# The low three bits of the weights: from VectorE to GpSimd

## The chip, the cores and the metric

The kernel runs on one core of one Trainium2 chip. The metric is the device time of one execution in microseconds (us). The engines are named as the profile names them: PE (TensorE, products), PEld (its weight loads), DVE (VectorE), ACT (ScalarE), POOL (GpSimd) and SP (SyncE, which here only issues the DMAs).

## What is computed

The reference reads the weights as float64 and everything else as float32. Cross-attention between 8 x 8 blocks of 512 tokens and 32 state slots comes first, then a feed-forward layer with a rational activation.

```python
scores = scale * np.matmul(x, state.transpose(0, 1, 3, 2))
a = np.exp(scores - scores.max(-1, keepdims=True)); a /= a.sum(-1, keepdims=True) + 1e-09
xread = np.matmul(a, state)                  # sread: the same with the roles exchanged
h = concat([xread, sread], 2) @ w_in         # w_in: 512 x 2048, float64
P = a0 + a1*h + a2*h**2 + a3*h**3
Q = 1 + |b0|*|h| + |b1|*h**2
out = (P / (Q + 1e-6)) @ w_out               # w_out: 2048 x 512, float64
```

[...]

## The kernel before, in words

The hidden width of 2048 is cut into 8 blocks (u = 0 to 7) of 256. Nine token blocks (b = 0 to 8: eight times 512 tokens, then the state rows) times 8 blocks of width give 72 steps n = 8b + u. The chain of one step is: PE makes h (token `F`, line 755); ACT and DVE make numerator and denominator (`FC` and `FB` on ACT, `mu`, `po` and `qd` on DVE, which read h in PSUM); ACT takes the reciprocal through a logarithm and an exponential (`qa`, `ln`, `ex`); DVE and POOL make the activation as a high and a low part (`g1`, `g2` and `g3` on DVE, `gl` on POOL); PE multiplies both with `w_out` (`mh`, `ml`, line 828).

The conversion of the weights takes place in the first 120 us or so, woven between steps 0 to 7. The 16 groups of raw weights are numbered k = 0 to 15: groups 0, 1, 2, 4, 6, 8, 10 and 12 are blocks of `w_in`, the others blocks of `w_out`. For each group the raw words are loaded (`lr`, SP), ACT makes `cv_y` (`cp`, line 325), DVE makes `cv_r` from the low words (`jr`, lines 333 to 342, in two halves of 512 columns for groups 0 to 4 and in one piece of 1024 after that), and DVE joins them (`jl`, line 351). A block of `w_in` goes into `win_sb`, from which PE makes the extra products `X` (line 659: state times `w_in`). Their results are copied out of PSUM by ACT (`XA`, `fA`) or DVE (`XV`) and stored. A block of `w_out` is split into a high part (cast by ACT, line 362) and a remainder, which POOL subtracts (`sp`, line 363; for groups 13 and 14 DVE does it, `sv`).

The order of the work is written out by hand: the list `ORDER` is a string of tokens, and each engine gets its instructions in the order of the tokens. Every engine works through its own list in order; an instruction that waits holds up all that stand behind it on that engine. The h tiles and the results of the extra products share two buffers in PSUM (`ps_h`, tag `h`), so an extra product can begin only when the tile two places before it has been read. The tag `cv` has four buffers for `cv_y` and `cv_r`, the tag `raw` two.

Around the conversion POOL has, in its order: the subtraction of the row maxima of batch 0 (`row_sup`, line 503), the row scaling (`row_norm`, line 544), the remainder of group 3 (`sp:3`), then `gl` of a step and `sp` of a group in turns, later the low part of the attention matrix (`a_lp`, line 574) and the split of the weights of the later steps (`fs`, line 708).

Of the kernel before, what the change touches and what calls it, by code (L numbers as in the profile page):

```python
# [183 lines left out]

class Tagged:


    def __init__(self, ctx, tc, bufs):  # L190
        self.bufs = bufs
        self.pools = {
            t: ctx.enter_context(tc.tile_pool(name=t, bufs=n)) for t, n in bufs.items()
        }

    def tile(self, shape, dtype, name, tag, bufs=None):
        return self.pools[tag].tile(shape, dtype, name=name, tag=tag)
# [3 lines left out]
def attention_rational_ffn(  # L201
# [22 lines left out]
    cp = ctx.enter_context(tc.tile_pool(name="cp", bufs=1))  # L224
    ld = ctx.enter_context(tc.tile_pool(name="ld", bufs=2))
    at = Tagged(
        ctx,
        tc,
        dict(e1=1, mx=2, sT=1, cm=2, rs=2, e2T=1, e2=1, r2=2, aT=2, sr=2),
    )  # L230
    cv = ctx.enter_context(tc.tile_pool(name="cv", bufs=4))
    ew = Tagged(ctx, tc, dict(xo=2, m=2, A=3, C=3, L=2, gh=2, gl=2))
    wp = ctx.enter_context(tc.tile_pool(name="wp", bufs=1))
    wo = wp.tile([P, 2, U * 2, DM], F32R, name="wo")
    ps_o = ctx.enter_context(tc.tile_pool(name="ps_o", bufs=1, space=PSUM))
    ps_h = ctx.enter_context(tc.tile_pool(name="ps_h", bufs=2, space=PSUM))
# [121 lines left out]
    def conv_split(k, eng):  # L358
        _, u = groups[k]
        m = CV[k][1].bitcast(F32)  # L360
        f = slice(2 * u, 2 * u + 2)
        nc.scalar.copy(wo[:, 0, f, :], m)  # L362
        eng.tensor_tensor(  # L363
            wo[:, 1, f, :], m, wo[:, 0, f, :].bitcast(F32), op=ALU.subtract
        )

    def load_win(n):
        t = ld.tile([P, NP, CW], F32, name="win_sb", tag="win", bufs=3)
        nc.sync.dma_start(t, w_in32[n % U])
        win_t[n] = t  # L370
# [74 lines left out]
    def col_max(b, j=None):  # L445
        cm = once(b, "cm", at_tile("cm", [P, 2], 2))
# [82 lines left out]
    def row_sum(b, j=None):  # L529
        rs = once(b, "rs", at_tile("rs", [P, NT * 8], 2))  # L530
# [136 lines left out]
    def extra_out(i, copy):  # L667
# [4 lines left out]
        else:  # L672
            t = ew.tile([P, 2, 2, CW], F32, name="xo", tag="xo", bufs=2)
# [18 lines left out]
    def load_m(n):  # L692
        t = cv.tile([P, 2, 2, CW], F32, name="m_sb", tag="raw", bufs=2)
# [10 lines left out]
    def fold_split(n):  # L704
# [115 lines left out]
    def mm(n, t, parts, place):  # L820
# [51 lines left out]
    def sread_hi():  # L872
        t = cv.tile([P, 2, NP, B * NS], F32R, name="sh", tag="raw", bufs=2)
# [7 lines left out]
    def keep_warm(k):  # L881
# [8 lines left out]
        "jr": join_rest,  # L890
        "jl": join_low,
# [4 lines left out]
        "fs": fold_split,  # L896
# [106 lines left out]
```

## Time and profile before

| | |
|---|---|
| median of 3 runs | 664.8 us (664.68 to 665.32) |
| span of the profiled execution, first to last instruction | 662.6 us |
| what lies around the span (median less span) | 2.2 us |
| PE busy | 645.4 us, 97% |
| DVE busy | 617.8 us, 93% |
| ACT busy | 513.4 us, 77% |
| POOL busy | 319.0 us, 48% |

The span is the profiled execution's own time between its first and last instruction; the time that a run reports also holds what lies around it. A busy engine is one that has an instruction under way. For PE the end of an instruction is a model, so that a busy PE need not be at its peak; a gap between its instructions is a real wait. A timeline row gives start, duration, engine, line, operation, output and inputs, and in brackets the idle time just before it with the engine that ended it.

### The profile page before, as it was taken

The page shows a single profiled execution, that of the slowest core. Times are in us where ns is not written, and L with a number is a line of the kernel's source. Part 1 is how long each engine was busy: PE and PEld are TensorE (multiplying, and loading weights), DVE is VectorE, ACT ScalarE, POOL GpSimd, SP SyncE. Part 2 cuts the span into 40 slices and gives each one's busy share as a digit, 9 for nine tenths or more (in the row PEclk, how much of TensorE's full clock was granted, in tenths as well). Part 3 has the DMA queues.
Part 4 walks back from the last instruction along what each step waited for, and adds up shares of the span by engine and source line. Part 5 has one row for each costly group of instructions (what it writes and reads, how often), then busy time and mean ns, then how long its engine had stood idle before and what let it go on. Part 6 is the DMA issues. An engine that isn't in the chain of part 4 may idle for free.

```text
span 662.6 us, 11126 instructions
## 1 busy us (share of the span) xinstructions
PE 645.4 (97%) x4442; PEld 504.8 (76%) x4442; DVE 617.8 (93%) x586; ACT 513.4 (77%) x604; POOL 319.0 (48%) x172
## 2 busy tenths in 40 slices
PE   5899999999999999999999999999999999999997
PEld 3355555778887888788887888787878888888995
DVE  5898899999989999999999999999999899999885
ACT  5888988887777888787778778787888678875663
POOL 1234442554654556645555454635545446464531
PEclk9999999999999999999999999999999999999999
DMA  8989897350330512132215022231225101111301
GB/s 332 393 304 355 303 344 264 125 190 8 105 113 20 187 48 96 32 121 83 71 43 180 13 96 63 86 138 33 95 81 174 33 0 48 63 48 65 97 1 63
DMA packets 28984, 81.46 MB, mean 123 GB/s; under 512 B 2820, under 2 KB 2948, under 8 KB 28932
## 3 DMA queue, kind: packets, MB, share of 16 engines
q1 hardware_dynamic: 28932, 80.75, 34.9%
q8 instruction: 35, 0.57, 0.3%
q14 instruction: 17, 0.14, 0.1%
HBM read 52.95 MB, written 27.79 MB: 122 GB/s over the span
## 4 chain that ended last, share of the span: by engine, by line
PE 84%; ACT 0%; DVE 0%; issue 0%
PE h L755 28%; PE o__1655 L828 2%; PE o__5714 L828 2%; PE o__1696 L828 2%; PE o__5193 L828 2%; PE o__3485 L828 2%; PE o__2273 L828 2%; PE o__4639 L828 2%; PE o__4009 L828 2%; PE o__2839 L828 2%; PE o__3455 L828 2%; PE o__2301 L828 2%; PE o__1681 L828 2%; PE o__5754 L828 2%; PE o__4014 L828 2%; PE o__2850 L828 2%
## 5 line engine op out<-in xcount | busy, mean ns | idle before, releaser
L818 POOL TENSOR_TENSOR gl<-C,L 128x1024 fp32r<-128x1024 f32 (+1 forms) x70 | 173.1, 2473 | 235.6 <-DVE C L811 155.9
L755 PE MATMUL h<-aT,m 128*128 128x512 f32 x736 | 193.4, 409 | 0.7 <-ACT xo L675 0.6
L755 PEld LDWEIGHTS h<-aT,m 128*128 128x128 f32 x736 | 137.2, 188 | 42.8 <-issue 12.2
L767 ACT ACTIVATE C<-h,cst 128x1024 f32<-128x1024 f32 (+1 forms) x72 | 83.2, 1156 | 47.6 <-PE h L755 35.6
L708 POOL TENSOR_TENSOR m<-m_sb,m 128x512 fp32r<-128x512 f32 x56 | 80.1, 1435 | 56.2 <-ACT m L707 37.4
L774 ACT ACTIVATE A<-h,cst 128x1024 f32<-128x1024 f32 (+1 forms) x72 | 76.7, 1065 | 30.6 <-PE h L755 26.3
L799 DVE SCALAR_TENSOR_TENSOR gh<-C,cst,L 128x1024 fp32r<-128x1024 f32 (+1 forms) x72 | 90.3, 1254 | 6.1 <-ACT L L870 2.3
L788 DVE SCALAR_TENSOR_TENSOR A<-A,b0a,h 128x1024 f32<-128x1024 f32 (+1 forms) x72 | 87.1, 1215 | 7.8 <-ACT A L774 6.6
L811 DVE SCALAR_TENSOR_TENSOR C<-C,cst,A 128x1024 f32<-128x1024 f32 (+1 forms) x72 | 89.4, 1241 | 2.2
L782 DVE SCALAR_TENSOR_TENSOR C<-C,cst,h 128x1024 f32<-128x1024 f32 (+1 forms) x72 | 87.7, 1219 | 2.1
L805 DVE SCALAR_TENSOR_TENSOR A<-A,gh 128x1024 f32<-128x1024 f32 (+1 forms) x72 | 87.7, 1218 | 1.7
L778 DVE TENSOR_TENSOR C<-C,h 128x1024 f32<-128x1024 f32 (+1 forms) x72 | 82.8, 1152 | 5.9 <-ACT C L767 4.0
L794 ACT ACTIVATE A<-A 128x1024 f32<-128x1024 f32 (+1 forms) x72 | 72.6, 1011 | 19.5 <-DVE A L788 19.5
L860 ACT ACTIVATE L<-A 128x1024 f32<-128x1024 f32 (+1 forms) x72 | 73.0, 1013 | 3.6 <-ACT A L794 0.4
L870 ACT ACTIVATE L<-L 128x1024 f32<-128x1024 f32 (+1 forms) x72 | 72.8, 1013 | 1.6
L659 PE MATMUL ps_x<-win_sb,st 64*32 64x256 f32 x1024 | 34.5, 388 | 4.2 <-DVE win_sb L351 2.5
L707 ACT CAST m<-m_sb 128x512 fp32r<-128x512 f32 x56 | 34.0, 613 | 0.1
L659 PEld LDWEIGHTS ps_x<-win_sb,st 64*32 64x32 f32 x1024 | 17.5, 107 | 17.2 <-issue 5.1
L755 PEld LDWEIGHTS h<-sh,m 128*128 128x128 f32 x192 | 24.2, 191 | 0.7
L755 PE MATMUL h<-sh,m 128*128 128x256 f32 x192 | 24.4, 283 | 0.0
L363 POOL TENSOR_TENSOR wo<-cv_r,wo 128x1024 fp32r<-128x1024 f32 x6 | 15.4, 2565 | 16.2 <-ACT wo L362 16.2
L544 POOL TENSOR_TENSOR e<-e,rs 128x512 f32<-128x512 f32 x13 | 13.9, 1085 | 12.4 <-DVE rs L538 12.4
(262 smaller groups left out, 1121.4 us busy)
## 6 DMA issues: line engine op xcount, KB each, us to landing
m_sb<-m_dram SPq DMA_DIRECT2D x28, 512.0 KB, 4.7
m_dram<-xo SPq DMA_DIRECT2D x20, 512.0 KB, 4.4
out_dram<-o_sb SPq DMA_DIRECT2D x34, 256.0 KB, 4.4
xT_sb<-in_xT_dram SPq DMA_DIRECT2D x16, 512.0 KB, 5.0
x_sb<-in_x_dram SPq DMA_DIRECT2D x16, 512.0 KB, 6.4
raw<-in_w_out_dram SPq DMA_DIRECT2D x14, 512.0 KB, 6.8
raw<-in_w_in_dram SPq DMA_DIRECT2D x12, 512.0 KB, 6.8
w_in_dram<-win_sb SPq DMA_DIRECT2D x8, 512.0 KB, 5.9
```

The source lines that it names most:

```text
L708: nc.gpsimd.tensor_tensor(m[:, 1], t, m[:, 0].bitcast(F32), op=ALU.subtract)
L755: nc.tensor.matmul(h[:, ci * W : (ci + 1) * W], l, r, start=(q == 0), stop=(q == len(seq) - 1),)
L767: nc.scalar.activation(e["C"], e["h"], AF.Identity, scale=cst[:, 3:4], bias=cst[:, 2:3])
L774: nc.scalar.activation(e["A"], e["h"], AF.Abs, scale=cst[:, 5:6])
L778: nc.vector.tensor_tensor(e["C"], e["C"], e["h"], op=ALU.mult)
L782: nc.vector.scalar_tensor_tensor(e["C"], e["C"], cst[:, 1:2], e["h"], op0=ALU.add, op1=ALU.mult)
L788: nc.vector.scalar_tensor_tensor(e["A"], e["A"], b0a, e["h"], op0=ALU.add, op1=ALU.mult)
L799: nc.vector.scalar_tensor_tensor(e["gh"], e["C"], cst[:, 0:1], e["L"], op0=ALU.add, op1=ALU.mult)
L805: nc.vector.scalar_tensor_tensor(e["A"], e["A"], 1.0 + 1e-6, e["gh"].bitcast(F32), op0=ALU.add, op1=ALU.mult)
L811: nc.vector.scalar_tensor_tensor(e["C"], e["C"], cst[:, 0:1], e["A"], op0=ALU.add, op1=ALU.subtract)
L818: eng.tensor_tensor(e["gl"], e["C"], e["L"], op=ALU.mult)
L828: nc.tensor.matmul(O[t], e[l][:, j * W + t * P : j * W + (t + 1) * P], wo[:, k, 2 * u + j, :], start=(place == FIRST[n // U, t] and i + j ...
```

## The change

All 21 tokens `jr` in `ORDER` become `jp`, at the same places in the string. `jp` calls the same function with `nc.gpsimd` as the engine. There the product with 2^-29 and the minimum with 7 become a product with 0.92 * 2^-29 and a sum with 0.139, which also ends at 7 when rounded. The tile `cv_r` of a group is now taken from the four `cv` buffers when its bits are made, and no longer when `cv_y` is. The rest of the diff moves the numbers of buffers into one table and adds a token (`ft`) that `ORDER` does not use.

```diff
-    "... row_exp:0:0 jr:0:1 lr:3 cp:1:1 ls:2:8 lr:2 col_max:0:1 "
+    "... row_exp:0:0 jp:0:1 lr:3 cp:1:1 ls:2:8 lr:2 col_max:0:1 "
...
+    def conv_tile(k, w):
+        if (k, w) not in CV:
+            CV[k, w] = cv.tile(
+                [P, 2, 2 * CW], I32, name=("cv_y", "cv_r")[w], tag="cv"
+            )
+        return CV[k, w]
+
     def conv_parts(k, j=None):
-        if k not in CV:
-            CV[k] = [
-                cv.tile([P, 2, 2 * CW], I32, name=name, tag="cv", bufs=4)
-                for name in ("cv_y", "cv_r")
-            ]
...
-    def join_rest(k, j=None):
+    def join_rest(k, j=None, eng=None):
         js = slice(0, 2) if j is None else slice(j, j + 1)
-        nc.vector.tensor_scalar(
-            CV[k][1][:, js],
+        (eng or nc.vector).tensor_scalar(
+            conv_tile(k, 1)[:, js],
             raw_words(k, j, 0),
-            2.0**-29,
-            7.0,
+            0.92 * 2.0**-29,
+            0.139,
             op0=ALU.mult,
-            op1=ALU.min,
+            op1=ALU.add,
         )
...
         "jr": join_rest,
+        "jp": lambda k, j=None: join_rest(k, j, nc.gpsimd),
```

In the listings of the order that follow, a line number of the kernel after is some 9 above that of the kernel before. POOL at the start, in the kernel before (`e_153` is the attention matrix of batch 0, `cv_r` and `wo` of the third row belong to group 3):

```order
L503 TENSOR_TENSOR e_153<-e_153,mx 128x512 x2
L544 TENSOR_TENSOR e_153<-e_153,rs 128x512 x2
L363 TENSOR_TENSOR wo<-cv_r,wo 128x1024
L818 TENSOR_TENSOR gl<-C,L 128x1024
L363 TENSOR_TENSOR wo<-cv_r,wo 128x1024
```

The same place after:

```order
L511 TENSOR_TENSOR e_153<-e_153,mx 128x512
L344 TENSOR_SCALAR cv_r<-raw 128x512 x2
L511 TENSOR_TENSOR e_153<-e_153,mx 128x512
L344 TENSOR_SCALAR cv_r<-raw 128x512 x2
L552 TENSOR_TENSOR e_153<-e_153,rs 128x512 x2
L344 TENSOR_SCALAR cv_r<-spare 128x512 x2
L372 TENSOR_TENSOR wo<-cv_r,wo 128x1024
L344 TENSOR_SCALAR cv_r<-spare 128x512 x4
L344 TENSOR_SCALAR cv_r<-raw 128x1024
L826 TENSOR_TENSOR gl<-C,L 128x1024
```

The two halves of group 3 stand ahead of the subtraction of group 3 (L372); the four halves behind it are those of group 2 and then of group 4, and the whole piece is group 5.

DVE at the same place, before (the first join is that of group 3, the second, into `win_sb`, that of group 2; `C` and `h` belong to step 0):

```order
L335 TENSOR_SCALAR cv_r<-spare 128x512 x2
L351 SCALAR_TENSOR_TENSOR cv_r<-cv_y,cv_r 128x1024
L335 TENSOR_SCALAR cv_r<-spare 128x512
L512 TENSOR_SCALAR r_200<-r_200 128x2
L516 RECIPROCAL r_200<-r_200 128x2
L335 TENSOR_SCALAR cv_r<-spare 128x512
L351 SCALAR_TENSOR_TENSOR win_sb<-cv_y,cv_r 128x1024
L778 TENSOR_TENSOR C<-C,h 128x1024
```

After:

```order
L360 SCALAR_TENSOR_TENSOR cv_r<-cv_y,cv_r 128x1024
L520 TENSOR_SCALAR r_199<-r_199 128x2
L524 RECIPROCAL r_199<-r_199 128x2
L360 SCALAR_TENSOR_TENSOR win_sb<-cv_y,cv_r 128x1024
L786 TENSOR_TENSOR C<-C,h 128x1024
```

The bits have left DVE, and the join of group 2 still stands ahead of the first product of step 0.

POOL near the end of the conversion, before (`m` is the first split of later weights, step 8; the last row is the subtraction of group 15):

```order
L818 TENSOR_TENSOR gl<-C,L 128x1024
L574 TENSOR_TENSOR aT<-eT,aT 128x1024
L708 TENSOR_TENSOR m<-m_sb,m 128x512
L818 TENSOR_TENSOR gl<-C,L 128x1024
L363 TENSOR_TENSOR wo<-cv_r,wo 128x1024
```

After (from the bits of group 13 on):

```order
L344 TENSOR_SCALAR cv_r<-raw 128x1024
L552 TENSOR_TENSOR e_857<-e_857,rs 128x512
L344 TENSOR_SCALAR cv_r<-raw 128x1024
L826 TENSOR_TENSOR gl<-C,L 128x1024
L344 TENSOR_SCALAR cv_r<-raw 128x1024
L582 TENSOR_TENSOR aT<-eT,aT 128x1024
L716 TENSOR_TENSOR m<-m_sb,m 128x512
L344 TENSOR_SCALAR cv_r<-raw 128x1024
L826 TENSOR_TENSOR gl<-C,L 128x1024
L372 TENSOR_TENSOR wo<-cv_r,wo 128x1024
```

The bits of groups 13, 12, 14 and 15 stand here, those of group 12 behind a row scaling and those of group 15 behind the split of step 8.

## Rows read from the trace of the kernel before

**Rows 1.** The page: busy time of PE over the whole span.

```profile
PE 645.4 (97%) x4442; PEld 504.8 (76%) x4442; DVE 617.8 (93%) x586; ACT 513.4 (77%) x604; POOL 319.0 (48%) x172
```

**Rows 2.** Stretches: length, then busy us and instructions by engine, granted PE clock, DMA.

```profile
20.00:120.00 100.00, 95.58 (x1223) 55.20 (x1211) 92.74 (x92) 88.58 (x102) 35.20 (x14) 0.98 0.87 320
120.00:640.00 520.00, 519.98 (x2895) 427.04 (x2894) 497.87 (x449) 403.64 (x471) 275.76 (x146) 1.00 0.24 80
```

**Rows 3.** The page's costliest groups: the extra products, idle before them by releaser.

```profile
L659 PE MATMUL ps_x<-win_sb,st 64*32 64x256 f32 x1024 | 34.5, 388 | 4.2 <-DVE win_sb L351 2.5
```

**Rows 4.** DVE by line: the bits, busy us and mean ns | idle before.

```profile
L335 DVE TENSOR_SCALAR cv_r<-raw 128x1024 int32<-128x1024 uint32 (+1 forms) x15 | 9.6, 643 | 0.6 <-DMA raw<-in_w_out_dram 0.4
L335 DVE TENSOR_SCALAR cv_r<-spare 128x512 int32<-128x512 uint32 x6 | 2.3, 416 | 0.0
```

**Rows 5.** Timeline of POOL, and one group of POOL by line.

```profile
0.24 0.10 POOL L983 MEMSET const-float32-0.0<- 128x1 f32 x1 [0.24 <-issue]
1.01 0.29 POOL masks.py:199 TENSOR_SCALAR_AFFINE_SELECT ident<-ident 128x128 f32<-128x128 f32 x1
7.38 1.05 POOL L503 TENSOR_TENSOR e<-e,mx 128x512 f32<-128x512 f32 x1 [6.08 <-DVE mx L495]
27.33 2.36 POOL L363 TENSOR_TENSOR wo<-cv_r,wo 128x1024 fp32r<-128x1024 f32 x1 [8.65 <-ACT wo L362]
...
L503 POOL TENSOR_TENSOR e<-e,mx 128x1024 f32<-128x1024 f32 x6 | 12.5, 2082 | 0.0
```

**Rows 6.** Timeline of DVE, 26 to 38 us.

```profile
26.35 1.22 DVE L778 TENSOR_TENSOR C<-C,h 128x1024 f32<-128x1024 f32 x1 [0.44 <-ACT C L767]
...
32.44 1.28 DVE L782 SCALAR_TENSOR_TENSOR C<-C,cst,h 128x1024 f32<-128x1024 f32 x1
33.64 0.75 DVE L335 TENSOR_SCALAR cv_r<-spare 128x512 int32<-128x512 uint32 x2
...
35.62 2.35 DVE L675 COPY xo<-ps_x 128x1024 f32<-128x1024 f32 x2
```

**Rows 7.** Timeline of PE, and its clock (the 1.00 or 0.50) at 31 us.

```profile
30.33 0.33 PE L592 MATMUL ps_sr__418<-x_sb,e2T 128*32 128x64 f32 x8 [1.95 <-ACT e2T L523]
...
31.62 1.96 PE L659 MATMUL ps_x<-win_sb,st 64*32 64x256 f32 x32
...
38.03 3.70 PE L755 MATMUL h<-aT,m 128*128 128x512 f32 x8
...
31.00:32.00 1.00, 1.00 (x32) 0.68 (x36) 1.00 (x2) 1.00 (x3) 0.00 (x0) 0.50 1.05 426
```

**Rows 8.** Timelines of DVE, POOL and PE, 94 to 100 us.

```profile
94.34 0.69 DVE L335 TENSOR_SCALAR cv_r<-raw 128x1024 int32<-128x1024 uint32 x1 [0.44 <-DMA raw<-in_w_out_dram]
...
98.21 1.23 DVE L351 SCALAR_TENSOR_TENSOR win_sb<-cv_y,cv_r 128x1024 int32<-128x1024 int32 x1
...
95.66 1.49 POOL L544 TENSOR_TENSOR e<-e,rs 128x512 f32<-128x512 f32 x1 [2.08 <-DVE rs L538]
...
99.58 1.10 PE L659 MATMUL ps_x<-win_sb,st 64*32 64x256 f32 x32 [0.37 <-DVE win_sb L351]
```

**Rows 9.** Timelines of POOL, DVE and PE, 117 to 131 us.

```profile
117.88 1.63 POOL L708 TENSOR_TENSOR m<-m_sb,m 128x512 fp32r<-128x512 f32 x1 [6.44 <-ACT m L707]
...
117.16 1.22 DVE L351 SCALAR_TENSOR_TENSOR cv_r<-cv_y,cv_r 128x1024 int32<-128x1024 int32 x1 [0.49 <-ACT cv_y L325]
118.31 2.29 DVE L811 SCALAR_TENSOR_TENSOR C<-C,cst,A 128x1024 f32<-128x1024 f32 x1
...
122.11 1.28 DVE L788 SCALAR_TENSOR_TENSOR A<-A,b0a,h 128x1024 f32<-128x1024 f32 x1 [0.38 <-ACT C L767]
...
125.69 2.47 DVE L782 SCALAR_TENSOR_TENSOR C<-C,cst,h 128x1024 f32<-128x1024 f32 x2
...
128.32 2.96 PE L755 MATMUL h<-aT,m 128*128 128x512 f32 x12
```

More of the change, by code (lines that the diff above doesn't have):

```diff
@@ L183, with __init__, tile @@
 ]
-class Tagged:
[L190 to L197, printed above, removed]
+TURNS = {}
+BUFS = dict(
+    e1=1, mx=2, sT=1, cm=2, rs=2, e2T=1, e2=1, r2=2, aT=2, sr=2, x=2, win=3, raw=2,
+    cv=4, xo=2, m=2, A=3, C=3, L=2, gh=2, gl=2, h=2,
+)
+class Tagged:
+    def __init__(self, pool, *tags):
+        self.pools = {t: pool(t) for t in tags} if tags else None
+        self.pool = None if tags else pool
+        self.turns = {t: iter(k) for t, k in TURNS.items()}
+    def tile(self, shape, dtype, name, tag):
+        pool = self.pools[tag] if self.pools else self.pool
+        return pool.tile(shape, dtype, name=name, tag=tag, bufs=BUFS[tag])
 @with_exitstack
@@ L222, in attention_rational_ffn, with pool @@
     T = S + NS
[L224 to L233, printed above, removed]
+    def pool(name, **kw):
+        return ctx.enter_context(tc.tile_pool(name=name, bufs=1, **kw))
+    cp = pool("cp")
+    ld = Tagged(pool("ld"))
+    at = Tagged(pool, "e1", "mx", "sT", "cm", "rs", "e2T", "e2", "r2", "aT", "sr")
+    cv = Tagged(pool("cv"))
+    ew = Tagged(pool, "xo", "m", "A", "C", "L", "gh", "gl")
+    wp = pool("wp")
     wo = wp.tile([P, 2, U * 2, DM], F32R, name="wo")
-    ps_o = ctx.enter_context(tc.tile_pool(name="ps_o", bufs=1, space=PSUM))
-    ps_h = ctx.enter_context(tc.tile_pool(name="ps_h", bufs=2, space=PSUM))
+    ps_o = pool("ps_o", space=PSUM)
+    ps_h = Tagged(pool("ps_h", space=PSUM))
     nc.scalar.preload_act_table_set("natural_log_exp_and_others")
@@ L281, in attention_rational_ffn @@
     XEARLY = {0: "C", 1: "C", 2: "C", 3: "A", 4: "A", 5: "A"}
-    BUFS = {"C": 3, "A": 3, "L": 2, "gh": 2, "gl": 2}
     def spare(tag, dtype):
-        return ew.tile([P, 2 * S], dtype, name="spare", tag=tag, bufs=BUFS[tag])
+        return ew.tile([P, 2 * S], dtype, name="spare", tag=tag)
     RAW, CV, win_t = {}, {}, {}
@@ L298, in load_raw @@
         elif (k, 0) not in RAW:
-            t = cv.tile([P, 2, 2 * CW, 2], U32, name="raw", tag="raw", bufs=2)
+            t = cv.tile([P, 2, 2 * CW, 2], U32, name="raw", tag="raw")
             RAW[k, 0], RAW[k, 1], RAW[k, None] = t[:, 0], t[:, 1], t
@@ L316, in raw_words @@
         return RAW[k, j][:, :, w].unsqueeze(1)
-    def conv_parts(k, j=None):
-        if k not in CV:
-            CV[k] = [
-                cv.tile([P, 2, 2 * CW], I32, name=name, tag="cv", bufs=4)
-                for name in ("cv_y", "cv_r")
-            ]
+    def conv_tile(k, w):
+        if (k, w) not in CV:
+            CV[k, w] = cv.tile(
+                [P, 2, 2 * CW], I32, name=("cv_y", "cv_r")[w], tag="cv"
+            )
+        return CV[k, w]
+    def conv_parts(k, j=None):
         js = slice(0, 2) if j is None else slice(j, j + 1)
         nc.scalar.activation(
-            CV[k][0][:, js].bitcast(F32),
+            conv_tile(k, 0)[:, js].bitcast(F32),
             raw_words(k, j, 1).bitcast(F32),
@@ L345, in join_low @@
         what, u = groups[k]
-        y, r = [t.rearrange("p j f -> p (j f)") for t in CV[k]]
+        y, r = [CV[k, w].rearrange("p j f -> p (j f)") for w in range(2)]
         w = r
         if what == "in":
-            win_t[u] = ld.tile([P, NP, CW], F32, name="win_sb", tag="win", bufs=3)
+            win_t[u] = ld.tile([P, NP, CW], F32, name="win_sb", tag="win")
             w = win_t[u].rearrange("p c f -> p (c f)").bitcast(I32)
@@ L359, in conv_split @@
         _, u = groups[k]
-        m = CV[k][1].bitcast(F32)
+        m = CV[k, 1].bitcast(F32)
         f = slice(2 * u, 2 * u + 2)
@@ L367, in load_win @@
     def load_win(n):
-        t = ld.tile([P, NP, CW], F32, name="win_sb", tag="win", bufs=3)
+        t = ld.tile([P, NP, CW], F32, name="win_sb", tag="win")
         nc.sync.dma_start(t, w_in32[n % U])
@@ L416, in once, with at_tile @@
         return T[key]
-    def at_tile(key, shape, bufs=None):
+    def at_tile(key, shape):
         def make():
-            kw = {"bufs": bufs} if bufs else {}
-            return at.tile(shape, F32, name=key, tag=key, **kw)
+            return at.tile(shape, F32, name=key, tag=key)
         return make
@@ L445, in col_max @@
     def col_max(b, j=None):
-        cm = once(b, "cm", at_tile("cm", [P, 2], 2))
+        cm = once(b, "cm", at_tile("cm", [P, 2]))
         nc.vector.tensor_reduce(
@@ L482, in col_exp @@
         e2 = once(b, "e2", at_tile("e2", [P, 2, S]))
-        r2 = once(b, "r2", at_tile("r2", [P, 2], 2))
+        r2 = once(b, "r2", at_tile("r2", [P, 2]))
         nc.scalar.activation(
@@ L493, in row_max @@
     def row_max(b, j=None):
-        mx = once(b, "mx", at_tile("mx", [P, NT * 8], 2))
+        mx = once(b, "mx", at_tile("mx", [P, NT * 8]))
         nc.vector.tensor_reduce(
@@ L529, in row_sum @@
     def row_sum(b, j=None):
-        rs = once(b, "rs", at_tile("rs", [P, NT * 8], 2))
+        rs = once(b, "rs", at_tile("rs", [P, NT * 8]))
         nc.vector.tensor_reduce(
@@ L550, in a_T @@
             if b not in AT:
-                AT[b] = at.tile([P, 2, 2, S], F32, name="aT", tag="aT", bufs=2)
+                AT[b] = at.tile([P, 2, 2, S], F32, name="aT", tag="aT")
             t = AT[b][:, 0]
@@ L568, in a_hi @@
         if b not in AT:
-            AT[b] = at.tile([P, 2, 2, S], F32R, name="aT", tag="aT", bufs=2)
+            AT[b] = at.tile([P, 2, 2, S], F32R, name="aT", tag="aT")
         (copy or nc.scalar.copy)(halves(b, AT[b][:, 0], j), turned(b, j))
@@ L601, in sr_copy @@
         T = TS[b]
-        T["sr"] = at.tile([P, 2, D], F32, name="sr", tag="sr", bufs=2)
+        T["sr"] = at.tile([P, 2, D], F32, name="sr", tag="sr")
         for j in range(2):
@@ L672, in extra_out @@
         else:
-            t = ew.tile([P, 2, 2, CW], F32, name="xo", tag="xo", bufs=2)
+            t = ew.tile([P, 2, 2, CW], F32, name="xo", tag="xo")
         XO[i] = t
@@ L692, in load_m @@
     def load_m(n):
-        t = cv.tile([P, 2, 2, CW], F32, name="m_sb", tag="raw", bufs=2)
+        t = cv.tile([P, 2, 2, CW], F32, name="m_sb", tag="raw")
         u = n % U
@@ L702, in load_m, with fold_split @@
             MF[n + k] = t[:, k]
-    def fold_split(n):
+    def fold_split(n, eng):
         t = MF.pop(n)
@@ L707, in fold_split @@
         nc.scalar.copy(m[:, 0], t)
-        nc.gpsimd.tensor_tensor(m[:, 1], t, m[:, 0].bitcast(F32), op=ALU.subtract)
+        eng.tensor_tensor(m[:, 1], t, m[:, 0].bitcast(F32), op=ALU.subtract)
     def fold_hi(n):
-        m = at.tile([P, 2, NP, CW], F32R, name="m2", tag="aT", bufs=2)
+        m = at.tile([P, 2, NP, CW], F32R, name="m2", tag="aT")
         nc.scalar.copy(m[:, 0], win_t[n])
@@ L765, in front_c @@
         e = EW[n]
-        e["C"] = ew.tile([P, 2 * S], F32, name="C", tag="C", bufs=3)[:, : e["N"]]
+        e["C"] = ew.tile([P, 2 * S], F32, name="C", tag="C")[:, : e["N"]]
         nc.scalar.activation(
@@ L772, in front_a @@
         e = EW[n]
-        e["A"] = ew.tile([P, 2 * S], F32, name="A", tag="A", bufs=3)[:, : e["N"]]
+        e["A"] = ew.tile([P, 2 * S], F32, name="A", tag="A")[:, : e["N"]]
         nc.scalar.activation(e["A"], e["h"], AF.Abs, scale=cst[:, 5:6])
@@ L824, in mm @@
         if place == FIRST[n // U, t]:
-            O[t] = ps_o.tile([P, DM], F32, name=f"o{t}_", tag=f"o{t}")
+            O[n // U, t] = ps_o.tile([P, DM], F32, name=f"o{t}_", tag=f"o{t}")
         for i, (l, k) in enumerate(parts):
@@ L828, in mm @@
                 nc.tensor.matmul(
-                    O[t],
+                    O[n // U, t],
                     e[l][:, j * W + t * P : j * W + (t + 1) * P],
@@ L842, in flush @@
     def flush(n, t, copy):
-        o = OS[n, t] = cv.tile([P, DM], F32, name="o_sb", tag="cv", bufs=4)
-        copy(o, O.pop(t))
+        o = OS[n, t] = cv.tile([P, DM], F32, name="o_sb", tag="cv")
+        copy(o, O.pop((n // U, t)))
     def store(n, t):
@@ L872, in sread_hi @@
     def sread_hi():
-        t = cv.tile([P, 2, NP, B * NS], F32R, name="sh", tag="raw", bufs=2)
+        t = cv.tile([P, 2, NP, B * NS], F32R, name="sh", tag="raw")
         for i in range(2):
@@ L895, in attention_rational_ffn @@
         "fV": lambda n: extra_first(n, nc.vector.tensor_copy),
-        "fs": fold_split,
+        "fs": lambda n: fold_split(n, nc.gpsimd),
+        "ft": lambda n: fold_split(n, nc.vector),
         "F": front,
```

32 rows, old and new, of the table ORDER are left out of this document.

## The prediction

> **What bounds the kernel now.** I read the busy times first: PE has an instruction under way for 645.4 of 662.6 us [rows 1]. The table by stretch then says where the rest is: between 120 and 640 us PE is busy for 519.98 of 520 us, between 20 and 120 us for 95.58 of 100 [rows 2]. So PE sets the end, and every microsecond that it waits is added to the time and never won back later. DVE is nearly as full in the first stretch (92.74 of 100 us), which is what the change relieves. But a full engine is not a bound: the column of releasers shows how little PE waits for it. The extra products wait 2.5 us in all for the joined weights (`win_sb`) from DVE [rows 3]. That is about what the relief could give. The timelines of POOL, DVE and PE were read last, at the places where a moved instruction now stands behind another.
>
> **What leaves DVE.** 15 instructions of 9.6 us and 6 of 2.3 us, 11.9 us in the first 117 us; a half takes 0.42 us and a whole piece (9.6 - 4 x 0.42) / 11 = 0.72 us [rows 4]. Little of it stands on PE's path, so I credit only what comes into the sums below.
>
> **What one costs on POOL.** The trace has no such operation on POOL. Above stand the two-input operations of the same width, 1.05 us for 512 columns and 2.08 us for 1024, and up to 1.49 and 2.36 us for single ones [rows 5, 8]. Below stands DVE's own time, 0.42 and 0.72 us [rows 4]. Nearest is POOL's only operation with one tensor input: 0.29 us for 128 columns, against 0.10 us for an instruction of one column [rows 5]. That makes 0.19/128 = 1.5 ns per column, so 0.10 + 512 x 1.5 ns = 0.86 us for a half and 1.62 us for a piece. I take these. The Trainium skill, GPSIMD Engine Reference, section "Engine selection", calls GpSimd roughly line-rate for one input, and its section "Elementwise — side-by-side cycle accounting" gives 769 ns measured for 512 elements; by that (an estimate) a half is 0.77 us, a piece 1.5 us, and the sum below some 0.6 us smaller. No row here shows which.
>
> **Where POOL's order makes others wait.** 21 short operations fit easily into an engine that is busy for 35.20 of 100 us [rows 2]. Their place is the matter: they keep DVE's place in the list, but on POOL other instructions stand in front, which themselves wait.
>
> *Groups 0 and 1.* Two halves follow `row_sup` (7.38 us, 1.05 us long) [rows 5], two more its second half. Each is 0.44 us longer than on DVE, but stands beside the loads of the raw weights and work that DVE still has. I take 0, with 4 x 0.44 = 1.8 us as the upper end.
>
> *Group 2, the main term.* On POOL its two halves stand behind the subtraction of group 3, which waits 8.65 us for ACT's cast and runs from 27.33 us for 2.36 us [rows 5]. ACT's cast stands behind step 0's h, so it does not come earlier. The halves can begin at 29.69 and end at 29.69 + 2 x 0.86 = 31.41 us. The join of group 2 (1.2 us) stands on DVE ahead of step 0's first product, `mu:0`, which so begins at 32.6 us instead of 26.35 [rows 6]. Everything behind it on DVE is 6.3 us late, and PE needs it: only DVE's reading of h frees the PSUM buffers into which PE puts its next extra products (31.62 us in the trace [rows 7]). In the trace those buffers come free with `po:1` at 32.44 + 1.28 us; then come the two halves of group 4 (0.75 us, now gone; with the gap behind them 0.84), a join, two copies until 35.62 + 2.35 = 37.97 us [rows 6], and PE's step 2 at 38.03 us [rows 7]. The same chain with 6.3 us more and 0.84 us less makes step 2 late by 6.3 - 0.84 = 5.4 us (rounded down). With POOL at DVE's speed it is 4.6 us (halves of 0.42), with halves of 1.49 us 6.7 us. ACT's next conversions wait too, but for the same event.
>
> *The clock there.* After a wait of 1.95 us PE's granted clock is 0.50 at 31 us, the lower of its two levels (1.2 GHz), and a batch of 32 extra products takes 1.96 us where the one at 99.58 us takes 1.10 [rows 7, 8]. A wait of 5 us more will keep it low for the batches that follow. I take one batch at the lower level, 1.0 us; the ends are 0 and three batches with step 2's eight products, some 6 us.
>
> *Groups 13 and 12.* The raw words of group 13 arrive at 94.34 us [rows 8]. POOL then makes its bits (to 95.96), the row scaling (1.05 to 1.49 us, to about 97.3) and only then the bits of group 12 (to 98.9 us). The join of group 12 began at 98.21 us, and PE already waited 0.37 us for it [rows 8]: 0.7 us more. At DVE's speed it is 0, with 1.49 and 2.36 us it is 2.3 us.
>
> *Group 15.* Its bits stand behind the split of step 8, which waits 6.44 us for ACT and runs from 117.88 to 119.5 us [rows 9]. They end at 121.1 us; the join began at 117.16 us. From the join to `qd:7` at 122.11 us DVE spends 4.95 us, of which 1.0 us is an operation that took 2.29 us instead of 1.28, and 0.38 us a wait [rows 9]; without these, 3.6 us. So `qd:7` comes at 124.7 us, 2.6 us late, and the second `po` behind it, which ended at 125.69 + 2.47 = 128.16 us, frees the buffer for PE's step 9 (128.32 us) [rows 9]. PE is late by 2.6 - 0.2 = 2.4 us; at DVE's speed 1.5 us, at the upper price 3.2 us.
>
> *What is hidden.* Groups 4 to 11 and 14 find POOL's list ready in time: in the places above DVE reaches the join later than POOL ends the bits. Loads wait for a raw buffer until POOL has read it, up to 1.6 us later; the loads in the queue behind have that much before ACT wants them. I cost both at nothing. If that cover fails, each group costs its 1.62 - 0.72 = 0.9 us.
>
> **Sum.** 5.4 + 1.0 + 0.7 + 2.4 = 9.5 us. The span becomes 672.1 us, and with the 2.2 us that lie around it 674.3 us. The profiled execution is not timed apart: the 2.2 us are the median of the runs, 664.8 us, less its span, and I leave them as they are.
>
> **Rivals.**
>
> *POOL and DVE shut each other out (677.3 us).* DVE's operation at 118.31 us, with two inputs from SBUF, took 2.29 us; POOL's split ran from 117.88 to 119.5 us, and what is left after its end is just the usual 1.28 us [rows 9]. If the bits shut out DVE for their whole length, eight pieces between 38 and 101 us cost 8 x 1.62 = 13.0 us less the relief of 8 x 0.72 = 5.8: 7.2 us. DVE's idle time in the stretch is 7.3 us [rows 2], which I let hide the larger half; 3.0 us come on top. Against it: most of DVE's operations of a step read PSUM. The Trainium skill, SBUF — State Buffer, section "Who interferes with whom", makes it a rule: a VectorE instruction with two SBUF inputs and a GpSimd instruction that reads SBUF exclude each other, and the one that comes second blocks fully. By it the row at 118.31 us is no accident, and the sum would be this rival's.
>
> *A slow operation (679.8 us).* The conversions from and to integers are in no row. At 1.49 and 2.36 us the terms are 1.8 + 6.7 + 1.0 + 2.3 + 3.2 = 15.0 us. For it: everything on POOL with 1024 columns takes over 2 us. Against it: one input, not two.
>
> *A quick operation (670.9 us).* At DVE's speed 4.6 + 1.5 = 6.1 us, with no clock term. For it: half as much is read as by POOL's two-input operations.
>
> *Faster (662.3 us).* The relief reaches PE: the 2.5 us for which the extra products wait for `win_sb` go [rows 3], and POOL's bits are always early. It decides at group 2: its bits must be there when DVE wants them for `mu:0` at 26.35 us, so by about 25 us. POOL would have to make them before the subtraction that runs until 29.69 us, and the order has them behind it.
>
> *No change (664.8 us).* The waits are there, but before stages in which PE would have waited anyway. Against it: PE has only 4.4 us of idle time in the 100 us [rows 2], most of it not at these places.
>
> **How the numbers follow.** Forecast 46%, POOL and DVE shutting each other out 16%, slow operation 14%, quick operation 14%, faster 6%, no change 4%. No change means within 0.2%, which is about what a measurement of this kernel can tell. So slower is 46 + 16 + 14 + 14 = 90%, same 4%, faster 6%. The forecast's own range, with halves of 0.6 to 1.05 us and a clock term of 0 to 3 us, is 672 to 677 us. The range for 8 in 10 leaves out the two last cases and a part of the slow one: 669 to 681 us.
>
> **What would show it.** In the profile of the changed kernel: a wait of DVE of about 6 us between 25 and 32 us, ahead of the join of group 2 and `mu:0`, released by POOL's bits; a wait of PE of about 5 us before the extra products at 31 us, and the lower clock after it; waits of DVE for POOL before the joins of groups 12 (near 108 us there) and 15 (near 126 us); a mean of the new operation on POOL of 0.86 and 1.62 us. The forecast is wrong if POOL's bits of group 2 end before 25 us, if PE's extra products at 31 us do not wait for DVE, or if PE is idle for under 9 us in its first 130 us.

## The result, and the profile after

The changed kernel takes 672.6 us (median of 4 runs, 671.6 to 675.6), beside 665.1 us for the kernel before: a ratio of 1.0115, 95% interval 1.0091 to 1.0139, so slower by 7.5 us. 674.3 us were forecast, with a range of 669 to 681. The profiled execution has a span of 669.8 us, 7.2 us more than before. In what follows the line numbers are those of each run's own kernel: the join is L360 after, and L359 in experiments with a string of `ORDER` one line shorter.

What was moved are the last three bits of the mantissa. The kernel makes a float32 out of each weight of 64 bits: ACT makes most of it from the high word (`cv_y`), the last three bits come from the low word (`cv_r`), and DVE joins the two with a shift and an or. A half is an operation over 512 columns, a piece one over 1024.

The busy times of the page answer to [rows 1]. PE has 1.8 us more, POOL 23 us more; DVE has only 4.1 us less, though 11.9 us of work left it:

```profile
PE 647.2 (97%) x4442; PEld 505.2 (75%) x4442; DVE 613.7 (92%) x565; ACT 513.6 (77%) x604; POOL 342.3 (51%) x193
```

The table by stretch answers to [rows 2] (length, then PE, PEld, DVE, ACT and POOL; the start of the second stretch is moved by 7.2 us):

```profile
20.00:127.20 107.20, 97.86 (x1231) 56.73 (x1219) 88.88 (x76) 91.26 (x104) 53.89 (x31) 0.97 0.80 297
127.20:647.20 520.00, 518.87 (x2887) 425.29 (x2887) 498.42 (x450) 401.97 (x470) 276.36 (x146) 1.00 0.25 80
```

PE's idle time in the first stretch grew from 4.4 to 9.3 us, and about 1 us of the place near the end of the conversion now lies in the second. So most of the loss is idle time of PE in the first 130 us, as forecast; 1.8 of the 7.2 us are busy time of PE, 0.7 of them in the first 20 us, where step 0 is not later for it (20.38 us in both). The page's group of the extra products says for whom it waits; in [rows 3] there were 4.2 us in all, and none for `A`:

```profile
L667 PE MATMUL ps_x<-win_sb,st 64*32 64x256 f32 x1024 | 34.6, 390 | 8.4 <-DVE A L796 4.8 <-DVE win_sb L360 2.5 <-ACT xo L683 0.3
```

**What the operation costs on POOL.** The groups of POOL's line (busy us, mean ns of one, idle before):

```profile
L344 POOL TENSOR_SCALAR cv_r<-raw 128x1024 int32<-128x1024 uint32 x11 | 15.4, 1398 | 0.9
L344 POOL TENSOR_SCALAR cv_r<-spare 128x512 int32<-128x512 uint32 x6 | 4.0, 658 | 1.8 <-DVE win_sb L360 1.3
L344 POOL TENSOR_SCALAR cv_r<-raw 128x512 int32<-128x512 uint32 x4 | 3.5, 885 | 0.8 <-DMA raw<-in_w_in_dram 0.6
```

0.66 us for a half; the single pieces at 102.31 and 124.31 us below take 1.14 and 1.16 us, so the means above that hold operations that were held up.

**The three places.** First group 2. POOL, DVE and PE, each from the timeline (start us, us, operation, idle time before and its releaser):

```profile
27.34 2.35 POOL L372 TENSOR_TENSOR wo<-cv_r,wo 128x1024 fp32r<-128x1024 f32 x1 [6.54 <-ACT wo L371]
29.78 1.38 POOL L344 TENSOR_SCALAR cv_r<-spare 128x512 int32<-128x512 uint32 x2
...
102.31 1.14 POOL L344 TENSOR_SCALAR cv_r<-raw 128x1024 int32<-128x1024 uint32 x1
...
122.96 1.27 POOL L716 TENSOR_TENSOR m<-m_sb,m 128x512 fp32r<-128x512 f32 x1 [4.88 <-ACT m L715]
124.31 1.16 POOL L344 TENSOR_SCALAR cv_r<-raw 128x1024 int32<-128x1024 uint32 x1
```

```profile
31.20 1.23 DVE L360 SCALAR_TENSOR_TENSOR win_sb<-cv_y,cv_r 128x1024 int32<-128x1024 int32 x1 [7.70 <-POOL cv_r L344]
32.34 1.21 DVE L786 TENSOR_TENSOR C<-C,h 128x1024 f32<-128x1024 f32 x1
...
103.49 1.23 DVE L360 SCALAR_TENSOR_TENSOR win_sb<-cv_y,cv_r 128x1024 int32<-128x1024 int32 x1 [1.03 <-POOL cv_r L344]
...
125.50 1.23 DVE L360 SCALAR_TENSOR_TENSOR cv_r<-cv_y,cv_r 128x1024 int32<-128x1024 int32 x1 [3.89 <-POOL cv_r L344]
```

```profile
30.34 0.32 PE L600 MATMUL ps_sr__418<-x_sb,e2T 128*32 128x64 f32 x8 [1.95 <-ACT e2T L531]
36.12 1.96 PE L667 MATMUL ps_x<-win_sb,st 64*32 64x256 f32 x32 [4.75 <-DVE A L796]
39.25 2.18 PE L667 MATMUL ps_x<-win_sb,st 64*32 64x256 f32 x64 [0.16 <-ACT m L688]
42.02 1.10 PE L667 MATMUL ps_x<-win_sb,st 64*32 64x256 f32 x32 [0.34 <-DVE xo L683]
43.16 3.70 PE L763 MATMUL h<-aT,m 128*128 128x512 f32 x8
...
104.86 1.10 PE L667 MATMUL ps_x<-win_sb,st 64*32 64x256 f32 x32 [0.77 <-DVE win_sb L360]
...
129.11 0.73 PE L836 MATMUL o__618<-wo,gh 128*128 128x512 f32 x2 [0.35 <-DVE wo L372]
131.38 0.73 PE L836 MATMUL o__618<-wo,gl 128*128 128x512 f32 x2 [0.60 <-POOL gl L826]
135.17 3.00 PE L763 MATMUL h<-aT,m 128*128 128x512 f32 x12
```

Read across: POOL's halves of group 2 begin where the subtraction of group 3 ends and finish at 31.16 us; DVE has waited 7.70 us for them and starts the join, then `mu:0` at 32.34 us (26.35 before [rows 6]); PE waits 4.75 us for the buffer that DVE frees, and step 2 is at 43.16 us (38.03 before [rows 7]): 5.1 us late. Then group 12: the products wait 0.77 us for `win_sb` instead of 0.37 [rows 8]. Then group 15: its bits stand behind the split of step 8, DVE waits 3.89 us, and step 9 comes at 135.17 us (128.32 before [rows 9]), 6.85 us late, where step 8 was 5.27 us late (125.39 against 120.12 us). From there to the end little is added: PE's last products start 7.1 us later than before.

### The profile page after: what moved, and what is told of

It reads as the page before. It is cut to its first block, busy times and chain, and to the rows that moved or that the text cites. A ratio compares the mean times of both kernels' runs of the same rounds, so it can differ in the third digit from the quotient of the medians.

```text
span 669.8 us, 11121 instructions
## 1 busy us (share of the span) xinstructions
PE 647.2 (97%) x4442; PEld 505.2 (75%) x4442; DVE 613.7 (92%) x565; ACT 513.6 (77%) x604; POOL 342.3 (51%) x193
## 4 chain that ended last, share of the span: by engine, by line
PE 82%; DMA 5%; DVE 4%; issue 4%; POOL 2%; ACT 2%; SPq 1%; DVEq 0%; POOLq 0%; ACTq 0%
PE h L763 28%; PE o__1655 L836 2%; PE o__5714 L836 2%; PE o__1696 L836 2%; PE o__3485 L836 2%; PE o__2273 L836 2%; PE o__5193 L836 2%; PE o__4009 L836 2%; PE o__2839 L836 2%; PE o__3455 L836 2%; PE o__2301 L836 2%; PE o__1681 L836 2%; PE o__5754 L836 2%; PE o__4014 L836 2%; PE o__5213 L836 2%
## 5 line engine op out<-in xcount | busy, mean ns | idle before, releaser
L807 DVE SCALAR_TENSOR_TENSOR gh<-C,cst,L 128x1024 fp32r<-128x1024 f32 (+1 forms) x72 | 92.7, 1288 | 5.8 <-ACT L L878 2.1
L796 DVE SCALAR_TENSOR_TENSOR A<-A,b0a,h 128x1024 f32<-128x1024 f32 (+1 forms) x72 | 87.2, 1216 | 6.8 <-ACT A L782 6.1
L372 POOL TENSOR_TENSOR wo<-cv_r,wo 128x1024 fp32r<-128x1024 f32 x6 | 15.4, 2570 | 10.8 <-ACT wo L371 10.7
L360 DVE SCALAR_TENSOR_TENSOR win_sb<-cv_y,cv_r 128x1024 int32<-128x1024 int32 x8 | 10.9, 1367 | 10.3 <-POOL cv_r L344 10.3
```

The costliest lines, as they stand in the source:

```text
L796: nc.vector.scalar_tensor_tensor(e["A"], e["A"], b0a, e["h"], op0=ALU.add, op1=ALU.mult)
L807: nc.vector.scalar_tensor_tensor(e["gh"], e["C"], cst[:, 0:1], e["L"], op0=ALU.add, op1=ALU.mult)
```

## The experiments

All but one of these kernels differ from the changed one in `ORDER` alone (the last one listed has another arithmetic); "back on DVE" writes `jr` for `jp`, which runs the same product and sum on DVE. The kernel before took 665.3 to 665.4 us in these comparisons. Theory A, B and C are the rival accounts of the texts written before each run.

**Group 2 back on DVE.**

```diff
-jp:2:1 lq:0:0 ... jp:2:0 jl:2
+jr:2:1 lq:0:0 ... jr:2:0 jl:2
```

> The changed kernel with the bits of group 2 alone back on DVE. Theory A (place in POOL's list: three groups stand behind POOL instructions that themselves wait): the wait of DVE ahead of step 0's first product goes, and with it the 5.1 us by which PE's step 2 came late (43.16 against 38.03 us). The waits for groups 12 and 15 stay (0.4 and 1.6 us). 672.6 - 5.1 = 667.5 us. Theory B (POOL and DVE shut each other out, all over the conversion): two of 21 operations go, which is a tenth of the loss: 671.8 us. Theory C (the new form or the later taking of a cv buffer costs the time on its own): 672.6 us.

Measured: 666.6 us, ratio 1.0016 (1.0005 to 1.0027). Two tokens give back 5.9 of the 7.5 us. Step 2 stands at 37.63 us. The places of groups 12 and 15 stay. The row of step 2, and the waits of DVE (us in total, times, longest):

```profile
37.63 3.70 PE L762 MATMUL h<-aT,m 128*128 128x512 f32 x8
...
DVE cv_r L359 <- POOL cv_r L343: 4.8, 2, 3.9
```

From step 7 to step 9 it takes 130.22 - 116.48 = 13.74 us, against 128.32 - 116.13 = 12.19 before.

**All bits on POOL, group 2 ahead of the subtraction.**

```diff
-sp:3 lr:9 jp:2:1 ... jp:2:0 jl:2
+jp:2:1 jp:2:0 sp:3 lr:9 ... jl:2
```

> The changed kernel with all bits on POOL, and the two halves of group 2 moved ahead of the subtraction of group 3 in the list. Theory A: as with group 2 on DVE, 667.5 us, and DVE idle for under 0.5 us ahead of step 0's first product. If POOL as the engine is the cause whatever the place (theory B), 672 us or more.

Measured: 666.9 us, ratio 1.0018 (1.0007 to 1.0030), the same as with group 2 on DVE, and step 2 at 37.23 us. DVE is idle for 1.41 us ahead of `mu:0`, not for under 0.5, but it waits there for ACT's copy of h and no longer for POOL, and `mu:0` begins at 26.19 us (26.35 before). So it is the place behind `sp:3` that costs, not that POOL makes the bits.

```profile
37.23 3.70 PE L762 MATMUL h<-aT,m 128*128 128x512 f32 x8
```

**Only group 2 on POOL, all others back on DVE.**

> All bits on DVE in the new form but those of group 2, which stay on POOL behind the subtraction of group 3. Theory A (place in POOL's list): one misplaced group costs nearly the whole loss, 5 to 6 us over the kernel with all bits on DVE (665.8 us), so 671 us. Theory B (POOL and DVE shut each other out): two half operations in a stretch where DVE stands still can cost under 1 us: 666.5 us.

Measured: 672.1 us, ratio 1.0094 (1.0079 to 1.0108). PE's timeline there shows the same wait:

```profile
36.05 1.96 PE L666 MATMUL ps_x<-win_sb,st 64*32 64x256 f32 x32 [4.64 <-DVE A L795]
39.17 2.96 PE L666 MATMUL ps_x<-win_sb,st 64*32 64x256 f32 x64 [0.15 <-ACT m L687]
...
43.94 3.70 PE L762 MATMUL h<-aT,m 128*128 128x512 f32 x8
```

**Only group 15 on POOL.**

> All bits on DVE in the new form but those of group 15, which stay on POOL behind the split of step 8. Theory A: PE's step 9 late by 1.6 us, 667.4 us, with DVE idle for some 3.5 to 4 us ahead of the join of group 15. Theory B: one operation, under 0.5 us: 666 us.

Measured: 667.3 us, ratio 1.0028 (1.0017 to 1.0040). DVE waits 4.2 us for POOL, and steps 7 to 9 take 130.90 - 117.10 = 13.80 us, 1.6 us more than before: the same loss as in the changed kernel, from this one instruction. The wait of DVE there (total, times, longest):

```profile
DVE cv_r L359 <- POOL cv_r L343: 4.2, 1, 4.2
```

**All bits on DVE, in the new form.** This leaves only the rest of the diff: the sum in place of the minimum and the tile taken later.

> The changed kernel with all bits back on DVE, but in the new form (product and sum) and with the buffer for them taken later. Theory A: 665.0 us, within 0.5 us of the kernel before. Theory C: the form or the order of the buffers is the cause, 670 us or more.

Measured: 665.8 us, ratio 1.0006 (0.9991 to 1.0021). The rest of the diff does nothing that can be told from the noise (the interval is 1 us to either side). On DVE the sum costs what the minimum did: 720 ns for a piece, where [rows 4] give 0.72 us.

```profile
L343 DVE TENSOR_SCALAR cv_r<-raw 128x1024 int32<-128x1024 uint32 x11 | 7.9, 720 | 0.9 <-DMA raw<-in_w_out_dram 0.9
```

**All bits on POOL, groups 2, 12 and 15 moved up.**

```diff
-sp:3 lr:9 jp:2:1 ... jp:2:0 jl:2
+jp:2:1 jp:2:0 sp:3 lr:9 ... jl:2
...
-row_norm:1:1 X:25 XA:25 jp:12 jl:12
+jp:12 row_norm:1:1 X:25 XA:25 jl:12
...
-X:31 lm:8 fs:8 XS:27 jp:15 jl:15
+X:31 jp:15 lm:8 fs:8 XS:27 jl:15
```

> The changed kernel with all bits on POOL and three groups moved up in the list: group 2 ahead of the subtraction of group 3, group 12 ahead of the row scaling, group 15 ahead of the split of step 8. Theory A: all three waits go, 672.6 - 5.1 - 0.4 - 1.6 = 665.5 us, between 664.5 and 666. Theory B: POOL and DVE still shut each other out, so at least 3 us of the loss stay: 668 us or more. If the relief of DVE is worth something once the waits are gone, it comes out under 664.5 us.

Measured: 664.5 us, ratio 0.9983 (0.9973 to 0.9992). The three moves take back the whole loss, and steps 2, 6 and 9 stand where they stood before (38.03, 100.61 and 128.32 us):

```profile
38.18 3.70 PE L762 MATMUL h<-aT,m 128*128 128x512 f32 x8
...
100.63 3.70 PE L762 MATMUL h<-aT,m 128*128 128x512 f32 x8
...
128.35 3.00 PE L762 MATMUL h<-aT,m 128*128 128x512 f32 x12
```

This is the best version of the study, but it is under the kernel before by only 0.17%. Twelve us of work have left DVE, and PE has next to nothing from it.

**The same, with groups 0 and 1 back on DVE.**

> The order with three groups moved up (664.5 us), and the four halves of groups 0 and 1 back on DVE, where PE's second batch of extra products waited 1.6 us for the join. If that wait counts, 663.9 us; if PE's step 0 is set by other work (it began at 20.5 us with that wait and at 20.38 without), no change, 664.5 us.

Measured: 665.6 us, ratio 1.0002 (0.9992 to 1.0011): no gain. Step 0 stands at 20.34 us, at 20.50 with these groups on POOL, so PE's wait of 1.6 us for the join is absorbed before step 0. That POOL is slower costs nothing there. The time is even 1.1 us longer than with these groups on POOL, which neither expectation allows; the two profiled executions (664.7 and 664.5 us) do not show that difference, and its cause is open.

**The same, every bit made twice on POOL.** Two identical operations where there was one.

```diff
-jp:2:1 jp:2:0 sp:3
+jp:2:1 jp:2:1 jp:2:0 jp:2:0 sp:3
```

> The order with three groups moved up (664.5 us), with every operation on the bits done twice on POOL: 21 more operations, 21 us more of POOL's time. Theory A: POOL has room, and only the two late groups wait for the second copy, 12 for about 2 us and 15 for about 1: 665 to 667 us. Theory B: each operation shuts out DVE, and doubling them doubles that: if it hides in DVE's slack now, it shows when doubled, 668 us or more.

Measured: 677.4 us, ratio 1.0175 (1.0158 to 1.0192), 13 us more than with the bits once. Theory A fell: POOL's idle time is not room. The number is that of theory B, but not all of it is theory B's mechanism, as the two next runs show. POOL's and DVE's timelines between 50 and 60 us:

```profile
51.70 7.37 POOL L344 TENSOR_SCALAR cv_r<-raw 128x1024 int32<-128x1024 uint32 x4
```

```profile
51.94 2.00 DVE L807 SCALAR_TENSOR_TENSOR gh<-C,cst,L 128x1024 fp32r<-128x1024 f32 x1 [0.18 <-ACT L L878]
53.97 2.03 DVE L813 SCALAR_TENSOR_TENSOR A<-A,gh 128x1024 f32<-128x1024 f32 x1
55.92 2.17 DVE L360 SCALAR_TENSOR_TENSOR win_sb<-cv_y,cv_r 128x1024 int32<-128x1024 int32 x1
58.02 2.13 DVE L819 SCALAR_TENSOR_TENSOR C<-C,cst,A 128x1024 f32<-128x1024 f32 x1
60.07 1.21 DVE L360 SCALAR_TENSOR_TENSOR cv_r<-cv_y,cv_r 128x1024 int32<-128x1024 int32 x1
```

Four operations of POOL take 1.84 us each instead of 1.14, four of DVE 2.0 to 2.17 us instead of 1.2 to 1.3, all with two inputs; the next of DVE, when POOL is done, takes 1.21 us again. They run nearly by turns: the eight operations take from 51.70 to 60.15 us, 8.45 us, where alone they would add up to 9.5. The two runs that follow take the doubling apart.

**Only groups 0 and 1 twice.**

> The kernel with the three bits moved up, and only the bits of groups 0 and 1 made twice (4 more operations). Theory A (in the run with all bits made twice the late start is a term of its own): step 0 begins about 4.5 us later and step 2 about 3.9 us later than with the bits once, nothing more is lost behind it, and the time is 664.5 + 3.9 = 668.4 us. Theory B (the late start would have been absorbed, and the loss is all mutual shutting out of POOL and DVE): 664.5 to 665.5 us.

Measured: 667.7 us, ratio 1.0033 (1.0013 to 1.0052), 3.2 us above the kernel with the bits once. Step 0 is 2.8 us late (23.30 us), and step 9 still is (131.18 us). So the late start is a term of its own, somewhat smaller than expected (3.2 us, not 3.9).

**Only groups 4 to 11 twice.** These are 9 more operations, two halves and seven pieces, not 10 as the expectation counts.

> The kernel with the three bits moved up, and only the bits of groups 4 to 11 made twice (10 more operations). Theory A (POOL and DVE shut each other out, and DVE has no slack left for it): DVE's operations with two inputs between 50 and 105 us take up to 2 us each, PE waits for DVE and POOL in this stretch, step 6 comes some 6 to 7 us later and the time is about 670.5 us. Theory B (POOL's room covers these groups, and the loss with all bits made twice came from the late start and the places near the end): 664.5 to 666 us.

Measured: 671.4 us, ratio 1.0109 (1.0073 to 1.0146), 6.9 us above the kernel with the bits once, and theory A's number. DVE's operations at 49.83 to 57.94 us are stretched to 1.92, 2.02, 2.16 and 2.13 us, and PE waits for what DVE and POOL make late, the longest time here:

```profile
101.94 1.96 PE L666 MATMUL ps_x<-win_sb,st 64*32 64x256 f32 x32 [3.01 <-DVE C L789]
```

Its profiled execution took 676.0 us, longer than the other three (670.7 to 672.0), so its positions are not compared with others. Of the 13 us of the full doubling, 3.2 belong to the start and 6.9 to groups 4 to 11. The remaining 2.9 us are a difference, with an uncertainty of over 2 us, and no run had their groups (2, 3 and 12 to 15) doubled alone; 1.6 of them stand between steps 7 and 9 in the fully doubled run (140.73 - 126.91 = 13.82 us against 12.18), where group 15 is.

**The changed kernel with the old arithmetic on POOL.**

```diff
-            0.92 * 2.0**-29,
-            0.139,
+            2.0**-29,
+            7.0,
             op0=ALU.mult,
-            op1=ALU.add,
+            op1=ALU.min,
```

> The changed kernel with the old arithmetic on POOL: a product and a minimum instead of a product and a sum, all else as in the changed kernel. Theory A (only the place in the order and POOL's speed matter, not which second operation is used): the operation takes 0.65 us for a half and about 1.15 us for a piece as in the changed kernel, and the time is 672.6 us, ratio 1.0115 within 0.002. Theory B (the sum was chosen because POOL's minimum is slower): the operation takes at least 20% longer, 0.8 and 1.4 us, step 2 comes another 0.3 us or more later and the time is 673.5 us or more.

Measured: 694.9 us, ratio 1.0439 (1.0415 to 1.0464), 22 us above the changed kernel. Both theories underrated it. POOL's groups in the first 150 us:

```profile
L343 POOL TENSOR_SCALAR cv_r<-raw 128x1024 int32<-128x1024 uint32 x11 | 44.9, 4078 | 0.9
...
L343 POOL TENSOR_SCALAR cv_r<-spare 128x512 int32<-128x512 uint32 x6 | 11.7, 1955 | 1.7 <-DMA m_dram<-spare 1.3
```

A half takes 1.96 us where the sum takes 0.66; pieces that nothing holds up take 3.69 to 3.75 us. PE's wait ahead of the extra products grows to 7.32 us, and waits for `win_sb` of 2.98 and 2.78 us come at the start and before step 6. Without the other arithmetic the change would cost 29 us.

## Why the prediction was right, and where its sizes were off

**Group 2, 5.4 us forecast, 5.1 measured.** The mechanism is shown: moving the two halves (or putting them back on DVE) takes it away, and putting them alone on POOL brings it back, with 672.1 - 665.8 = 6.3 us against the kernel with all bits on DVE, 5.1 us of it at step 2 (43.94 against 38.83 us); the profiled spans differ by 5.7 us. The chain was right to a tenth: `mu:0` is 5.99 us late, less the 0.84 us that left DVE behind it makes 5.15, and step 2 is 5.13 late. Only the price of a half was off. One link was named wrongly: `po:1` frees the second of the two buffers; the first, for which PE waited 4.75 us, comes free with `qd:0` (`A`, L796). Both came late by the same wait, so the sum does not change.

**The price of the operation, 0.86 and 1.62 us forecast, 0.66 and 1.15 measured.** This is the step that failed in size. I took the slope of a mask operation over 128 columns. Between half and piece the new operation has a slope of (1.15 - 0.66) / 512 = 0.96 ns per column, not 1.5. The 769 ns of the Trainium skill (GPSIMD Engine Reference, "Elementwise — side-by-side cycle accounting") were nearer, but above every undisturbed half of the sum; and they are no price for the minimum, which took 1.96 us. My bounds did not hold the minimum either: 1.96 us for a half lies above the 1.49 of the slow rival (whose sum also kept the 1.8 us of groups 0 and 1 at the forecast's price; at its own they are 4.3). Which second operation the instruction has was nowhere in the working, and it decides about 22 us.

**The clock, 1.0 us forecast, about 0 measured.** The wait did bring the lower level, as the stretch shows (columns as above, the granted clock is the third from the end):

```profile
33.00:39.00 6.00, 2.88 (x64) 1.52 (x64) 5.93 (x6) 2.90 (x3) 1.91 (x3) 0.50 0.46 184
```

But the first batch behind it took 1.96 us in the kernel before as well, at the same level [rows 7]. The second, of 64 products, took 2.18 us against 1.96 before, and 2.96 us with only group 2 on POOL. None of this reached step 2: the last batch ahead of it waited for DVE's copy anyway (0.34 us, and 0.42 with only group 2). So 0.2 to 1.0 us of time was lost to the clock and about 0 on the path. (From the rows that the term was taken from, one batch is 1.96 - 1.10 = 0.86 us rather than 1.0.)

**Groups 12 and 15, 0.7 and 2.4 us forecast, 0.4 and 1.6 measured.** Both waits come at the joins that were named, that of group 12 at 103.49 us rather than near 108, and both shrink with the price. Group 15 is shown by itself (1.6 us); group 12 is read from its row, since no run had it alone.

**The sum.** 5.1 + 0 + 0.4 + 1.6 = 7.1 us; the span grew by 7.2. The 2.3 us by which the forecast was too high are the two terms of price and clock: 1.0 us of clock, the rest the price in three places.

**Hidden groups, forecast at nothing.** With the three moves the time is that of before, so groups 0, 1, 3 to 11, 13 and 14 cost nothing on balance on POOL: whether a small loss is hidden there by a small gain, no run shows. But the cover is thin, and not POOL's idle time: the doubling of groups 4 to 11 cost 6.9 us, that of groups 0 and 1 3.2.

**The rival of mutual shutting out** was put at 16% and 3 us. It happens, and costs PE nothing on balance as long as the bits are made once. In the first 128 us, the operation that makes `gh` took 1618 ns after (7 of them), and 1278 ns with all bits on DVE; the joins 1367 and 1483 ns instead of 1220 and 1217 (8 each), the operation of `A` 1338 instead of 1221 (7). That is 2.4 + 1.2 + 2.1 + 0.8 = 6.5 us of DVE's time, more than half of the 11.9 us that left it, and explains most of why the busy time of DVE fell by only 4.1 us. Not all of it ran beside the bits. `gh` and `A` did (3.2 us), and so did two short operations with one input (`rs` and `cm`, 1.9 us more). The joins' 3.3 us fell mostly beside operations that POOL had before as well, 2.1 us of it on one join:

```profile
65.33 1.24 POOL L344 TENSOR_SCALAR cv_r<-raw 128x1024 int32<-128x1024 uint32 x1
115.68 2.39 POOL L582 TENSOR_TENSOR aT<-eT,aT 128x1024 fp32r<-128x1024 f32 x1
```

```profile
65.48 2.17 DVE L807 SCALAR_TENSOR_TENSOR gh<-C,cst,L 128x1024 fp32r<-128x1024 f32 x1
115.80 3.35 DVE L360 SCALAR_TENSOR_TENSOR cv_r<-cv_y,cv_r 128x1024 int32<-128x1024 int32 x1
```

In the kernel before, the subtraction `aT` and the split of step 8 held up two other operations of DVE by 2.1 us (one of them the 2.29 us of [rows 9]); after, these were free of it. In both pairs DVE's operation begins just behind POOL's and ends 1.1 us after it. The rule of the Trainium skill (SBUF — State Buffer, "Who interferes with whom") that the second one blocks fully agrees with them; in the stream of the doubled run it is not quite full, 1.84 us for one and 2.0 to 2.17 us for the other where full turns would take 2.4. The row from which the prediction drew the rival leaves 1.1 us after the end of the split too, not 1.28.

**The faster case** fell where it was put: POOL ended group 2 at 31.16 us, not by 25. And when the order was mended, the gain was 0.17%. The extra products wait for `win_sb` 2.5 us in the changed kernel as before, and 1.7 of these stand behind joins that waited for POOL's bits (groups 1 and 12). With the three bits moved up one such wait is left, 1.63 us for group 1, and taking it away by putting groups 0 and 1 back on DVE gained nothing.

## What to carry to other kernels

Work moved to an idle engine keeps its place in the list but gets other neighbours: look at what stands ahead of it there and for whom that waits, before its duration. Two tokens in the wrong place cost 5.9 us here; the same work in the right place cost nothing and gave 0.17%. That so little came of it fits two readings, which no run separates: PE waited little for DVE's busy time, and more than half of what left DVE came back in operations that POOL held up. Measure the exact form of an operation on the engine that it moves to: the two forms that cost the same on DVE differ threefold on POOL.

## What the runs showed of the hardware

- POOL takes 0.66 us for a product and a sum over 512 columns, and 1.96 us for a product and a minimum; on DVE both take 0.42. Why the minimum is slow there the runs don't show.
- POOL's operation on the bits and DVE's operations with two inputs run nearly by turns, each taking 1.84 to 2.17 us where it takes 1.14 to 1.28 alone.
- The same wait of PE of 1.95 us at about 30.3 us was followed by a lower clock in some kernels and not in others. The stretch from 32 to 33 us, first with the three bits moved up, then with group 2 back on DVE:

```profile
32.00:33.00 1.00, 1.00 (x28) 0.19 (x15) 0.96 (x2) 1.00 (x3) 0.57 (x1) 0.50 1.11 447
```

```profile
32.00:33.00 1.00, 1.00 (x56) 0.59 (x40) 0.96 (x2) 1.00 (x2) 0.74 (x1) 1.00 1.03 422
```

The 32 products behind the wait took 1.63 us in the one and 1.09 in the other. So a step that follows such a wait moves by some half a microsecond to a whole one between kernels that are alike up to there (step 2 at 38.18 us with the three bits moved up, at 37.23 with group 2 alone moved up), and the positions of step 2 above are to be read with that in mind.
